# Float32 pair transposes, eight-step tap tiles, merged spectral products and a new order in a one-core convolution and MLP kernel

## The chip, the cores and the metric

The kernel runs on one core of a Trainium2 chip. The metric is the device time of one execution in microseconds. Three runs of the kernel before gave 232.59, 232.85 and 233.19, a median of 232.85.

The engines that matter are TensorE (PE in the profile; its weight loads are PEld), VectorE (DVE), ScalarE (ACT), GpSimd (POOL) and the DMA queue that SyncE (SP) issues. TensorE writes only to the accumulators in PSUM; DVE and ACT bring the results from there into SBUF, which is called evicting.

## The reference

The inputs have 2,048 time steps and 640 channels. The first layer is a convolution block, the second an MLP; both add to their input.

```python
x = A_q
h = x + _A_ref(_layernorm(x, axis=-1), A_k, A_v, A_shift_k, A_ssm_k, A_ssm_D)
h2 = h + _B_ref(_layernorm(h, axis=-1), B_w1, B_b1, B_w2)
# _A_ref: k_shift = sum over 4 taps of k, delayed by 0..3 steps, times shift_k
#         kv = k_shift * v
#         y = causal convolution of kv with ssm_k over the whole length (by FFT) + kv * ssm_D
#         return q * y                  # q is the normalized x
# _B_ref: h = x @ w1 + b1 (1,728 wide); act = h * tanh(softplus(h)); act @ w2
```

## The kernel before, in words

The work is written as named operations (`OP`, `DMA`), each with an engine or a choice of engines, the operations it needs and the buffers it takes. `ORDER` (line 26) is one list of all of them, each with its engine: t is TensorE, a ScalarE, v VectorE, p GpSimd, d the DMA queue of SyncE. `_schedule` (line 141) walks that list with planned durations and gives every operation a planned start; the instructions are then emitted in the order of these starts. So on each engine and on the DMA queue they run strictly in that order, whatever is ready. The planned durations decide only the order.

A time step t is 16*t1 + t2. The 640 channels are five blocks of 128, and three chunks: chunk 0 is block 0, chunk 1 blocks 1 and 2, chunk 2 blocks 3 and 4. The FFT is done as matmuls:

- `k1pe`/`k1ev` (lines 537, 543): each block of the filter is transposed, 16 transposes of 128x128 in bf16, and evicted to `kk_s`. `dadd` adds the D term to it.
- `ktpe`/`ktev`/`ktsh` (493 to 506): k is transposed for the tap convolution, 16 transposes a block, evicted in one operation, and GpSimd copies a shifted edge.
- `wsh` (418): GpSimd builds the tap matrices out of `coef`, which four VectorE casts bring from the matmul `cfpe`.
- `kspe` (512): the tap convolution, per block and half of the time 16 matmuls, eight of 128 columns and eight of 96. `kv` (524) multiplies its PSUM result by v on VectorE and writes `kv_all`.
- `s1k`, `s1v` (456): the first step of the transform of filter and of kv, 20 groups each, evicted as 1,024 columns (`s1kev`, `s1vev`).
- `s2k` (569) and `s2v` (605): the second step with the table `G`, 22 and 20 groups, evicted to `uk` (the filter's spectrum K) and `uv` (the spectrum V).
- `sw` (584): DMAs that swap neighbouring partitions of K into `SW` buffers, which lie in `xa`, `rn` and `rb`.
- `p2`, `p1` (621): VectorE or GpSimd multiplies SW by V in place and then V by K in place, 20 pairs.
- `i1` (656): the inverse transform's first step, 20 groups of 16 matmuls with V and SW as weights, evicted to `Z`, which lies in `uk`. The group of a chunk needs all products of that chunk.
- `i2` (720): the second step, per tile of 128 time steps; `y` evicts it, `wb` multiplies by the normalized x (`lnx`), `h` adds x, `bn`/`pow`/`hc` are the second LayerNorm, `trpe`/`trev` transpose it.
- `ln1`, `ln1p` (695, 702): statistics of the first LayerNorm, per tile two statistics operations, an aggregate and an addition of epsilon on VectorE, and a power and a scaling on GpSimd.
- `m1`/`hb` (786, 802) and `m2`/`res`/`d_out` (812 to 829): the MLP in units of 256, 256, 512, 512 and 512 steps, Mish on ScalarE with its result in `uv`, the residual on VectorE, and the output's DMA. The last tile goes in two halves of 320 columns (832 to 836).

PSUM is four tiles of two banks (`R_PS`): a matmul group takes one, and it comes free when its eviction has ended. `d_id` (379) is the loading of small constants over ScalarE's own queue; `warm` (383) is a Mish activation on two elements, which brings ScalarE's function table.

Of the kernel before, what the change touches and what calls it, by code (L numbers as in the profile page):

```python
# [11 lines left out]
ALU = mybir.AluOpType  # L12
# [4 lines left out]
S = 2048  # L17
D = 640
# [6 lines left out]
EPS = 1e-5  # L25
ORDER = """
cz:v d_id:a wz:v wm:t cfpe:t coef:v d_off:d d_n0:d k1pe0:t d_n2:d k1pe2:t k1ev0:v dadd0:v s1kpe0_0:t k1ev2:v s1kev0_0:a dadd2:v s1kpe0_1:t s1kev0_1:a
s1kpe0_2:t s1kev0_2:v d_n3:d k1pe3:t k1ev3:a dadd3:p d_n1:d k1pe1:t s1kpe2_2:t d_k0:d k1ev1:v s1kpe2_0:t d_k1:d s1kev2_2:a d_n4:d d_k3:d s1kpe2_1:t
s1kev2_1:a d_k2:d s1kpe0_3:t s1kev2_0:v s1kpe3_3:t s1kev3_3:a s1kpe2_3:t d_x0:d s1kev0_3:v s1kev2_3:a dadd1:v s1kpe3_2:t d_g0:d s1kpe3_0:t s1kev3_0:a
s1kpe1_2:t s1kev3_2:v s1kpe1_0:t s1kpe1_1:t k1pe4:t s1kev1_1:a s1kev1_2:v k1ev4:a dadd4:p ktpe1_0:t ktpe1_1:t s1kev1_0:v d_g1:d d_g3:d ktpe1_2:t  # L30
ktpe1_3:t ktev1:v s1kpe1_3:t s1kev1_3:a s1kpe3_1:t s1kev3_1:a d_g4:d w2z:p s1kpe4_0:t s1kpe4_2:t s1kev4_2:a ln1_0:v s1kev4_0:v s1kpe4_1:t s1kev4_1:a
s1kpe4_3:t s1kev4_3:a ktpe0_0:t d_g2:d ktpe0_1:t d_g7:d ktpe0_2:t ktpe0_3:t ktpe3_0:t ktpe3_1:t ktpe3_2:t wsh2:p d_v1:d ln1_3:v ktpe3_3:t wsh1:p
ln1_2:v ktev3:v ktev0:a ktpe4_0:t s2kpe_2:t s2kev_2:a ktpe4_1:t ktpe4_2:t ktsh0:p ktpe4_3:t ktev4:v ktsh3:p s2kpe_9:t ktsh1:p s2kev_9:a d_g5:d
s2kpe_10:t s2kev_10:v s2kpe_0:t s2kev_0:a s2kpe_1:t s2kev_1:a s2kpe_12:t kz:p s2kev_12:v d_v0:d s2kpe_6:t d_a12:d s2kev_6:a ktsh4:p s2kpe_5:t
s2kpe_3:t s2kev_3:a s2kev_5:v ktpe2_0:t ktpe2_1:t d_g6:d ktpe2_2:t ktpe2_3:t ktev2:v s2kpe_21:t wsh0:p s2kpe_8:t s2kev_21:a s2kpe_7:t ln1p0:p ln1p3:p
kspe1_1:t wsh3:p s2kev_8:a s2kpe_4:t s2kpe_19:t s2kev_7:v s2kev_4:a s2kev_19:a kspe2_1:t kv1_1:v s2kpe_11:t kv2_1:v s2kev_11:a sw0_0:d s2kpe_15:t
ktsh2:p s2kev_15:a kspe4_1:t kv4_1:v s2kpe_14:t s2kev_14:a sw1_0:d kspe2_0:t s2kpe_13:t s2kev_13:a s2kpe_16:t kspe1_0:t kv2_0:v s1vpe2_0:t s2kev_16:a
s1vev2_0:a kv1_0:v s1vpe2_2:t s1vev2_2:v s1vpe2_3:t s1vev2_3:a s1vpe1_0:t s1vev1_0:v s1vpe1_3:t s1vev1_3:a s1vpe1_2:t s1vev1_2:a s1vpe1_1:t s1vpe2_1:t
s1vev2_1:a s2kpe_20:t s1vev1_1:v s2kpe_17:t s2kev_17:a s2kev_20:v kspe3_0:t s2kpe_18:t s2vpe1_2:t kspe0_1:t s2kev_18:a s2vev1_2:a sw1_1:d p2_1_2:p
s2vpe1_1:t s2vev1_1:a kv3_0:v s2vpe1_3:t s2vev1_3:a kspe4_0:t ln1_1:v s2vpe1_4:t s2vev1_4:a kv0_1:v kv4_0:v p2_1_3:v s2vpe1_6:t s2vev1_6:a kspe0_0:t  # L40
s2vpe1_0:t s2vev1_0:a p1_1_2:v p1_1_3:p kv0_0:v kspe3_1:t d_x2:d warm:a kv3_1:v sw0_1:d s2vpe1_7:t s2vev1_7:a s1vpe4_1:t s1vev4_1:a p2_1_1:v p2_1_0:v
p1_1_1:v p1_1_0:p s1vpe3_2:t s1vev3_2:a s1vpe0_2:t s1vev0_2:a s1vpe4_0:t s1vev4_0:v s1vpe0_0:t s1vev0_0:a s1vpe3_0:t sw2_0:d s1vev3_0:v p2_1_7:v
s1vpe0_3:t s1vev0_3:a s1vpe0_1:t s1vev0_1:a s1vpe3_1:t s1vev3_1:v s1vpe4_2:t s1vev4_2:a s1vpe3_3:t s1vpe4_3:t s1vev4_3:a s1vev3_3:v s2vpe0_3:t
s2vev0_3:a p1_1_7:p p2_1_6:v sw2_1:d s2vpe2_4:t s2vev2_4:a s2vpe1_5:t s2vev1_5:a s2vpe0_1:t s2vev0_1:a p1_1_6:v p2_1_4:v s2vpe0_0:t p2_0_3:v
s2vev0_0:a p1_1_4:v p1_0_3:v p2_1_5:v p1_1_5:v s2vpe2_0:t p2_0_1:v p1_0_1:v s2vpe2_6:t s2vev2_6:a s2vpe2_5:t s2vev2_5:a s2vev2_0:v s2vpe0_2:t
s2vpe2_3:t s2vev0_2:a i1pe1_4:t s2vev2_3:a i1ev1_4:a s2vpe2_1:t p2_2_0:v p2_0_0:v s2vpe2_7:t s2vev2_7:a s2vpe2_2:t d_w14:d d_w10:d i1pe1_1:t
s2vev2_1:a i1ev1_1:a s2vev2_2:a i1pe1_7:t d_w12:d p1_0_0:v p2_0_2:v p1_0_2:v i1pe0_0:t i1ev0_0:a i1pe0_1:t i1ev0_1:a i1pe0_3:t p2_2_6:v i1ev0_3:a
p2_2_3:v p1_2_3:v p2_2_5:v p1_2_5:v p2_2_1:v p1_2_0:v p1_2_1:v p1_2_6:v i1pe0_2:t d_x1:d i1pe1_5:t p2_2_7:v p1_2_7:v d_w11:d i1ev0_2:a i1pe1_0:t
p2_2_4:v d_w13:d p1_2_4:v i1ev1_7:a i1ev1_5:a i1pe1_3:t i1ev1_3:a d_t2m:d i1ev1_0:a i1pe1_2:t p2_2_2:v p1_2_2:v i1pe1_6:t d_w2:d i1ev1_2:v i1pe2_5:t
i1pe2_7:t ln1_6:v d_small:p i1ev1_6:a gate:p lnx3:a i1ev2_5:a ln1p2:p ln1p1:p ln1_7:v i1ev2_7:a i1pe2_1:t i1ev2_1:a i1pe2_4:t i1ev2_4:v ln1_4:v  # L50
i1pe2_2:t i1ev2_2:a i1pe2_0:t i1ev2_0:a lnx1:p i1pe2_3:t i1ev2_3:v lnx2:p ln1p7:p ln1p6:p lnx6:p i1pe2_6:t ln1_12:v i2pa0:t i2pb0:t i2pa1:t ln1p4:p
i2pb1:t i1ev2_6:a lnx0:p i2pc1:t y1:a i2pc0:t y0:v lnx4:p b1pe:t wb1:v i2pa12:t i2pb12:t c_b1:a i2pc12:t y12:a wb0:v h0:v bn0:v i2pa3:t i2pb3:t
i2pc3:t y3:a i2pa2:t i2pb2:t i2pc2:t h1:p bn1:v i2pa6:t pow0:p hc0:v i2pb6:t y2:a i2pc6:t y6:a i2pa8:t i2pb8:t i2pc8:t y8:a i2pa11:t i2pb11:t i2pc11:t
y11:a i2pa5:t i2pb5:t i2pc5:t y5:a i2pa4:t i2pb4:t i2pc4:t y4:a i2pa13:t i2pb13:t i2pc13:t y13:a i2pa15:t i2pb15:t i2pc15:t y15:a pow1:p trpe0:t hc1:v
wb2:v i2pa7:t trev0:a i2pb7:t trpe1:t i2pc7:t trev1:v y7:a wb3:v i2pa10:t i2pb10:t i2pc10:t y10:a m1pe0_0:t m1pe0_2:t hb0_0:a m1pe0_4:t hb0_4:a
hb0_2:a h2:v bn2:v h3:p bn3:v pow2:p hc2:v m1pe0_1:t hb0_1:a pow3:p hc3:v m1pe0_6:t wb4:v h4:p trpe2:t trpe3:t lnx7:a trev2:v m1pe0_3:t hb0_6:a
ln1_10:v bn4:v ln1_5:v m1pe0_5:t wb7:p h7:p trev3:a m1pe1_1:t m1pe1_3:t wb6:v hb0_3:a h6:v hb1_1:a hb0_5:a ln1p5:p bn6:v m1pe1_4:t lnx5:a pow4:p bn7:v
hb1_3:a wb5:v h5:v bn5:v hb1_4:a m1pe1_6:t hb1_6:a pow7:p pow6:p hc4:v hc6:v hc7:v m2pe0:t trpe4:t trev4:a trpe6:t ln1_8:v trev6:a ln1p8:p ln1p10:p
ln1_11:v m1pe1_0:t ln1p11:p trpe7:t trev7:a res0:v pow5:p hb1_0:a hc5:v lnx10:a wb10:v h10:v m2pe1:t trpe5:t trev5:v m1pe1_5:t lnx11:a m1pe2_2:t
lnx8:a wb8:p h8:p wb11:v h11:v bn11:v res1:v m1pe2_0:t bn8:v pow8:p hc8:v hb2_2:a ln1_15:v ln1p15:p hb1_5:a ln1p12:p lnx12:p bn10:v pow10:p wb12:p  # L60
lnx15:p m1pe2_6:t h12:v bn12:v hb2_6:a m1pe2_5:t hb2_5:a m1pe1_2:t hb2_0:a hb1_2:a m1pe2_3:t hb2_3:a pow12:p ln1_13:v ln1p13:p i2pa9:t pow11:p i2pb9:t
i2pc9:t y9:a m1pe2_1:t hb2_1:a m1pe2_4:t hb2_4:a ln1_9:v ln1p9:p hc11:v lnx13:a lnx9:a wb9:v h9:p trpe8:t trev8:v bn9:v pow9:p m2pe2:t res2:v d_out2:d
trpe11:t d_out0:d hc9:v m2pe3:t res3:v m2pe7:t hc10:v trev11:a res7:v d_out7:d trpe10:t trev10:a trpe9:t trev9:v hc12:v ln1_14:v ln1p14:p lnx14:p
d_out1:d m2pe4:t res4:v d_out4:d wb15:v h15:p bn15:v i2pa14:t i2pb14:t i2pc14:t y14:a d_out3:d wb14:v h14:p m2pe6:t m1pe3_0:t bn14:v pow14:p m1pe3_2:t
res6:v d_out6:d wb13:v h13:v hb3_0:a hb3_2:a bn13:v m1pe3_1:t hb3_1:a trpe12:t m1pe3_5:t hc14:v hb3_5:a pow13:p pow15:p trev12:v m1pe3_6:t hb3_6:a
hc13:v hc15:v trpe15:t trev15:v m1pe3_3:t hb3_3:a trpe14:t trev14:v trpe13:t trev13:a m2pe5:t res5:v d_out5:d m1pe3_4:t hb3_4:a m1pe4_5:t hb4_5:a
m1pe4_4:t hb4_4:a m1pe4_1:t hb4_1:a m1pe4_2:t hb4_2:a m1pe4_3:t hb4_3:a m2pe8:t res8:v d_out8:d m1pe4_6:t hb4_6:a m1pe4_0:t hb4_0:a m2pe10:t m2pe14:t
res14:v d_out14:d res10:v d_out10:d m2pe12:t res12:v m2pe11:t res11:v m2pe13:t res13:v d_out13:d d_out12:d m2pe9:t res9:v d_out9:d d_out11:d m2ape15:t
resa15:v d_outa15:d m2bpe15:t resb15:v d_outb15:d
# [60 lines left out]


_SWITCH = 0.14
_COUNT = [('s1.pe|kspe|k1pe|i1pe', 32), ('ktpe', 8), ('s2kpe_21', 4), ('s2kpe', 12), ('s2vpe0', 64), ('s2vpe1', 32), ('s2vpe2', 32), ('i2pa', 4), ('i2pb', 4), ('i2pc', 8), ('wm', 20), ('trpe', 10), ('m1pe._6', 30), ('m1pe', 20), ('m2pe', 56), ('m2.pe', 28), ('cfpe|b1pe', 2)]
_MARK, _BLOCK, _FETCH, _SLOW = 204, 253, 2.2, 5.0
_PORT_DVE = r"(p[12]_|wsh|dadd|wb|h\d|hc)"
_PORT_POOL = r"(wsh|lnx|ktsh|dadd|p[12]_|wb|h\d|hc|ln1p|pow)"
# [69 lines left out]
def _make_tables():  # L206
# [13 lines left out]
    for dl in range(4):  # L220
        G[0, :, dl, :, 0, :, dl] = c
        G[1, :, dl, :, 0, :, dl] = -s
        G[0, :, dl, :, 1, :, dl] = -s
        G[1, :, dl, :, 1, :, dl] = -c
    T["g"] = np.moveaxis(G, 4, 6).reshape(128, 128 * 128)

    th = 2 * np.pi * g[:, None] * t2[None, :] / 16
    cg, sg = np.cos(th), np.sin(th)
# [648 lines left out]
```

## Time and profile before

| | us |
|---|---|
| median of three runs | 232.85 |
| profiled execution, its own time | 232.84 |
| its span in the profile | 231.1 |
| last spectral product ends (VectorE) | 84.26 |
| last i1 eviction ends (ScalarE) | 92.83 |
| first m1 matmul starts | 101.79 |
| last residuals start | 227.58 |

| engine | busy us | share of the span |
|---|---|---|
| PE | 219.0 | 95% |
| DVE | 145.0 | 63% |
| ACT | 137.8 | 60% |
| POOL | 69.6 | 30% |

A row of a group gives the line, the engine, the operation, what it writes and reads, and behind the bar the busy time, the mean duration in ns and the idle time before it. A duration runs from start to acknowledged end; a second operation right behind it begins a little before that end, so a row's mean is longer than the pace. The granted TensorE clock is 1.00 in every stretch. The 1.74 us between the span and the execution's own time lie outside the profile.

### The profile page before, as it was taken

To read this page: it belongs to the slowest core of one execution; us is meant where nothing else is said; L and a number is where in the kernel's file an instruction comes from. 1 tells how busy PE (TensorE), PEld (TensorE's weight loads), DVE (VectorE), ACT (ScalarE), POOL (GpSimd) and SP (SyncE) were. 2 spreads that over 40 slices of the span, in tenths; PEclk is the share of its full clock that TensorE was granted. 3 is DMA by queue.
4 is the path that set the end of the run, shared out by engine and by line. 5 is a ranking of instruction groups with operands and counts; after the bars stand their busy time and mean duration, and the time that the engine had idled before them with its cause. 6 is when DMAs were issued, how large, how long until landed. Compare 5 with 4: busy or idle time off the path is not lost.

```text
span 231.1 us, 6508 instructions
## 1 busy us (share of the span) xinstructions
PE 219.0 (95%) x2835; PEld 167.3 (72%) x2835; DVE 145.0 (63%) x277; ACT 137.8 (60%) x187; POOL 69.6 (30%) x98
## 2 busy tenths in 40 slices
PE   7999999997889989989999999999999999999993
PEld 2898999897789979878876455777446546577772
DVE  0888999899999998987997837554641100104121
ACT  2399999999999997887745586111355254300000
POOL 0002993036620039446547186305320000000000
PEclk9999999999999999999999999999999999999999
DMA  6999997437966299200000000012000000001012
GB/s 216 380 353 375 427 413 238 129 109 244 291 175 223 54 414 373 84 1 3 0 0 3 1 0 3 24 53 96 19 11 3 28 0 0 31 0 57 3 58 85
DMA packets 19215, 28.74 MB, mean 124 GB/s; under 512 B 1137, under 2 KB 15602, under 8 KB 18802
## 3 DMA queue, kind: packets, MB, share of 16 engines
q1 hardware_dynamic: 18896, 28.17, 34.7%
q8 instruction: 22, 0.36, 0.6%
q10 hardware_dynamic: 194, 0.15, 0.2%
q14 instruction: 7, 0.06, 0.1%
q0 software_dynamic: 96, 0.00, 0.0%
HBM read 20.45 MB, written 2.62 MB: 100 GB/s over the span
## 4 chain that ended last, share of the span: by engine, by line
PE 71%; DVE 18%; ACT 5%; issue 4%; POOL 0%; DVEq 0%
PE ps L818 26%; PE ps L797 25%; ACT uv L372 4%; DVE uv L374 3%; DVE uv L625 3%; DVE uk L374 3%; PE ps L496 2%; DVE rb L629 2%; PE ps L573 2%; PE ps L540 2%; PE ps L762 2%; PE ps L394 2%; PE ps L660 2%; PE ps L661 2%; PE ps L466 2%
## 5 line engine op out<-in xcount | busy, mean ns | idle before, releaser
L818 PE MATMUL ps<-rn,uv 128*128 128x320 bf16 x448 | 62.3, 299 | 0.0
L797 PE MATMUL ps<-G 128*128 128x512 bf16 (+1 forms) x325 | 58.3, 336 | 0.0
L806 ACT ACTIVATE uv<-ps,b1s 128x512 bf16<-128x512 f32 (+1 forms) x70 | 36.7, 592 | 35.7 <-PE ps L797 28.1
L818 PEld LDWEIGHTS <-uv 128*128 128x128 bf16 x448 | 43.5, 98 | 16.9
L372 ACT CAST uk<-ps 128x1024 bf16<-128x1024 f32 (+2 forms) x47 | 43.9, 1061 | 9.0 <-PE ps L467 6.4
L797 PEld LDWEIGHTS <-G 128*128 128x128 bf16 x325 | 31.4, 98 | 23.0 <-issue 0.4
L372 ACT CAST uv<-ps 128x1024 bf16<-128x1024 f32 x32 | 30.2, 1072 | 0.3 <-PE ps L467 0.3
L824 DVE TENSOR_TENSOR xa<-ps,xa 128x640 bf16<-128x640 f32 x6 | 4.9, 823 | 26.7 <-PE ps L818 26.7
L660 PE MATMUL ps<-a,uv 128*128 128x128 bf16 x160 | 18.7, 219 | 1.2 <-DVE uv L625 1.1
L660 PEld LDWEIGHTS <-uv 128*128 128x128 bf16 x160 | 17.9, 113 | 1.3 <-DVE uv L625 1.3
L824 DVE TENSOR_TENSOR xb<-ps,xb 128x640 bf16<-128x640 f32 (+1 forms) x7 | 4.9, 727 | 21.9 <-PE ps L818 21.9
L374 DVE CAST uk<-ps 128x1024 bf16<-128x1024 f32 (+1 forms) x15 | 17.6, 1197 | 1.0 <-PE ps L661 0.6
L749 POOL TENSOR_TENSOR r<-ve,mhalf 128x1 f32<-128x1 f32 x16 | 9.3, 585 | 15.1 <-DVE ve L746 15.1
L703 POOL TENSOR_TENSOR r<-ve,mhalf 128x1 f32<-128x1 f32 x16 | 9.0, 562 | 14.4 <-DVE ve L699 14.4
L609 PE MATMUL ps<-uv,G 128*128 128x64 bf16 (+1 forms) x384 | 12.4, 186 | 1.0 <-issue 0.7
L466 PE MATMUL ps<-cst,ra 128*64 128x128 bf16 x160 | 10.7, 219 | 2.4 <-ACT uv L372 1.3
L525 DVE TENSOR_TENSOR ra<-ps,rb 128x1024 bf16<-128x1024 f32 x10 | 12.0, 1222 | 1.3 <-PE ps L520 1.3
L609 PEld LDWEIGHTS <-G 128*128 128x128 bf16 x384 | 11.6, 96 | 1.3 <-issue 1.1
L372 ACT COPY G<-ps 128x640 bf16<-128x640 bf16 x8 | 5.5, 698 | 11.6 <-PE ps L762 11.6
L372 ACT CAST rb<-ps 128x640 bf16<-128x640 f32 x15 | 9.4, 726 | 4.9 <-PE ps L724 4.9
L625 DVE TENSOR_TENSOR uv<-uv,uk 128x1024 bf16<-128x1024 bf16 x17 | 11.5, 690 | 0.8
L573 PE MATMUL ps<-uk,G 128*128 128x160 bf16 x128 | 10.8, 230 | 0.2
(111 smaller groups left out, 384.2 us busy)
## 6 DMA issues: line engine op xcount, KB each, us to landing
G<-tab_g SPq DMA_DIRECT2D x8, 512.0 KB, 8.2
rn<-in_A_ssm_k_dram SPq DMA_DIRECT2D x5, 512.0 KB, 6.7
ra<-in_A_k_dram SPq DMA_DIRECT2D x4, 640.0 KB, 9.2
rb<-in_A_v_dram SPq DMA_DIRECT2D x2, 1280.0 KB, 14.4
G<-in_B_w_dram SPq DMA_DIRECT2D x5, 432.0 KB, 4.6
rn<-in_B_w_dram SPq DMA_DIRECT2D x1, 2080.0 KB, 12.3
rn<-uk SPq DMA_DIRECT2D x4, 512.0 KB, 4.0
rb<-uk SPq DMA_DIRECT2D x4, 512.0 KB, 8.0
```

The lines of the kernel that those rows point to most:

```text
L372: nc.scalar.copy(o, i)
L374: nc.vector.tensor_copy(o, i)
L466: nc.tensor.matmul(ps[0:64, dgl, :], lhs, mc, start=True, stop=True)
L525: nc.vector.tensor_tensor(kv_w[:, m, :, 8 * h:8 * h + 8, :], rt.tile.rearrange("p (l t d) -> p d t l", l=4, t=8), raw_v[:, 8 * h:8 * h + 8 ...
L573: nc.tensor.matmul(ps[:, o:o + 160], g_v[:, f, :], KA[:, :, f, :], start=True, stop=True)
L609: nc.tensor.matmul(ps[:, fl * st:fl * st + n], g_v[:, f0 + fl, :], V[c.i][:, :, f0 + fl, :], start=True, stop=True)
L625: eng.tensor_tensor(v, v, K[c.i][:, :, f0:f1, :], ALU.mult)
L660: nc.tensor.matmul(pz[:, dgl, :], V[c.i][:, dg // 4, :, dg % 4], a12[:, 0, :], start=True, stop=False)
L797: nc.tensor.matmul(ph[:, i * 512:i * 512 + w], w1[:, dc, fc * P:fc * P + P], lnhT_of(u)[:, dc, 0:w], start=(dc == 0), stop=(dc == NDC - 1))
L806: nc.scalar.activation(hb_of(u)[:, fc, 0:n], rt.tile[:, i * 512:i * 512 + n], ACT.Mish, bias=b1s[:, fc:fc + 1], scale=1.0)
L818: nc.tensor.matmul(po[:, a * 512:a * 512 + 320], hb_of(u)[:, fc, o - x * w // 2:o - x * w // 2 + P], w2[:, fc + x, a * 320:a * 320 + 320], ...
L824: nc.vector.tensor_tensor(x, rt.tile[:].rearrange("p (a d) -> p a d", a=2)[:, n, 0:320], x, ALU.add)
```

## The change

- The filter and k are transposed as float32 words that hold two bf16 neighbours: eight transposes for a block, with a float32 identity `eye`, where there were 16. The filter's pairs are two neighbouring steps; those of k are two neighbouring channels. The columns of `kk_s` and of kv become channel-major with the 16 steps innermost, and the rows of `G` follow.
- The tap tiles are 8 steps by 16 channels. `wsh` becomes five operations of 2x704 elements, one for each block, and lies beside `kt_s` in `uv`. `kspe` has matmuls of 128 and 48 columns, written to every second PSUM column. The shifted copy is two columns further left in the same buffer, so `ktsh` is gone. `coef` comes from six matmuls.
- `uk`, `xa`, `rn`, `rb` and `G` become parts of one tile `mega`. K and SW of a chunk so have one distance, and one operation multiplies both by V, read twice. The products stand in K and SW; V is left free. `i1` reads K and SW, `Z` lies in `uv`, and Mish's result in `uk`.
- `warm` comes first on ScalarE; the constants' queue has two more loads (`eye`, `rep`).
- `ln1` is without the addition of epsilon, which is done with the powers for batches of 2, 2, 4, 4 and 4 tiles.
- On tiles 0 and 1 `wf` reads i2's PSUM result and multiplies it by `lnx` in one operation.
- The last tile goes in pieces of 320, 224 and 96 columns. The load of x's last part no longer needs kspe.
- The order of everything is new. VectorE's list is, up to the last product: cz wz coef k1ev3 k1ev2 dadd1 s1kev0_0 s1kev3_1 s1kev2_0 s1kev0_2 k1ev4 s1kev3_2 ln1_3 ln1_0 s1kev1_2 ktev2 ln1_2 ktev1 ktev0 ln1_1 ktev4 ktev3 kv0_1 kv1_1 kv2_0 kv4_0 kv2_1 kv1_0 kv3_0 kv0_0 kv3_1 s1vev1_0 s2kev_3 s1vev2_0 s1vev1_1 kv4_1 p2_1_4 p2_1_6 s1vev0_3 s1vev3_1 s1vev3_3 s1vev0_1 p2_1_7 s2vev1_1 p2_1_2 s2vev1_3 p2_1_1 p2_1_3 p2_1_0 p2_2_5 p2_0_2 p2_0_3 p2_0_0 p2_0_1 and the other seven of chunk 2. ScalarE begins with d_id warm k1ev0 k1ev1 and then s1kev. TensorE has k1pe0, 3, 1 and 2 ahead of the first s1kpe. The DMA queue: n0 n3 n1 n2 g7 k3 g5 n4 k0 k2 x0 k1 a12 g6 g4 g3 v1 v0 g2 g1 g0, the six sw, x2.

```diff
+    sizes = [P * 160, 4096, NT * D + 1024, NT * D, P * P]
+    mega = big.tile([P, offs[5]], BF16, name="mega")
+    uk, xa, rn, rb, gt = [mega[:, offs[i]:offs[i + 1]] for i in range(5)]
...
-        Z.append(k.rearrange("p (j d) -> p j d", d=c.w))
+        KP.append(mega[:, a:a + 2 * d].rearrange("p (z o) -> p z o", z=2)[:, :, 0:P * c.ng].rearrange("p z (b f g) -> p z b f g", f=P, g=4))
+        Z.append(uv[c.i].rearrange("p (j d) -> p j d", d=c.w))
...
-                for gl in range(4):
-                    nc.tensor.transpose(ps[:, gl, a, :], raw_k[:, a * 4 * D + b * 4 + gl:(a + 1) * 4 * D:20], ident)
+                for l in range(2):
+                    c = 4 * h * D + 10 * r + 2 * b + l
+                    nc.tensor.transpose(ps[:, l, r, h, :], raw_k.bitcast(F32)[:, c:(h + 1) * 4 * D:20], eye[:])
...
-                    for a in (2 * h, 2 * h + 1):
-                        o = ps[:, l * 256 + (a - 2 * h) * P:][:, 0:P]
-                        nc.tensor.matmul(o, t[:, l, a, :], wsh[r // 5][:, r % 5, 0:128], start=True, stop=False)
-                        nc.tensor.matmul(o[:, 0:96], t[:, l, a - 1 if a else 4, :], wsh[r // 5][:, r % 5, 128:224], start=False, stop=True)
+                    for r in range(2):
+                        nc.tensor.matmul(ps[:, l * 256 + r:l * 256 + 256:2], t[:, l // 2, r, h, 8:136, l % 2], wsh[m][:, r, l, 0:128], start=True, stop=False)
+                        nc.tensor.matmul(ps[:, l * 256 + r:l * 256 + 96:2], t[:, l // 2, r, 1 - h, 8 - (1 - h):136 - (1 - h), l % 2], wsh[m][:, r, l, 128:176], start=False, stop=True)
...
-                nc.vector.tensor_tensor(kv_w[:, m, :, 8 * h:8 * h + 8, :], rt.tile.rearrange("p (l t d) -> p d t l", l=4, t=8),
-                                        raw_v[:, 8 * h:8 * h + 8, :, 4 * m:4 * m + 4].rearrange("p t d l -> p d t l"), ALU.mult)
+                nc.vector.tensor_tensor(kv_w[:, m, :, :, 8 * h:8 * h + 8], rt.tile.rearrange("p (l t d) -> p d l t", l=4, t=8),
+                                        raw_v[:, 8 * h:8 * h + 8, :, 4 * m:4 * m + 4].rearrange("p t d l -> p d l t"), ALU.mult)
...
-            for t2 in range(NT):
-                nc.tensor.transpose(ps[:, t2, :], n[:, t2:S:16], ident)
+            for t2 in range(8):
+                nc.tensor.transpose(ps[:, t2, :], n.bitcast(F32)[:, t2:S // 2:8], eye[:])
...
-                    eng.tensor_tensor(v, v, K[c.i][:, :, f0:f1, :], ALU.mult)
-                    return
-                for b, t in SW[c.i]:
-                    k = t[:, :, f0:f1, :]
-                    eng.tensor_tensor(k, k, v[:, b:b + t.shape[1]], ALU.mult)
+                kp = KP[c.i][:, :, :, f0:f1, :].rearrange("p z b f g -> p z b (f g)")
+                v = V[c.i][:, :, f0:f1, :].rearrange("p b f g -> p b (f g)").unsqueeze(1).to_broadcast([P, 2, c.ng // 4, 4 * (f1 - f0)])
+                (nc.gpsimd if e == "pool" else nc.vector).tensor_tensor(kp, kp, v, ALU.mult)
...
+            if fused:
+                nc.vector.tensor_tensor(v(tt_rt.tile), rt.tile[:, 0:D].rearrange("p (b d l) -> p b d l", b=5, l=4), v(lnx_rt.tile), ALU.mult)
+                return
```

## Prediction before the run

> **What bounds the kernel now.** I read the page's totals and slices first, then the busy times in chosen stretches, then the chain that ended last in order of time, then the groups with their shapes kept apart, and last the VectorE and ScalarE timelines for the pace of one operation behind another.
>
> ```profile
> span 231.1 us, 6508 instructions
> PE 219.0 (95%) x2835; PEld 167.3 (72%) x2835; DVE 145.0 (63%) x277; ACT 137.8 (60%) x187; POOL 69.6 (30%) x98
> ```
>
> ```profile
> 30.00:40.00 10.00, 9.85 (x161) 9.52 (x160) 9.00 (x9) 9.20 (x12) 6.49 (x8) 1.00 0.87 319
> 40.00:50.00 10.00, 9.58 (x250) 8.98 (x248) 9.01 (x12) 9.42 (x11) 0.41 (x1) 1.00 0.33 92
> ...
> 70.00:80.00 10.00, 9.86 (x195) 9.49 (x192) 9.69 (x15) 10.00 (x13) 0.00 (x0) 1.00 0.46 144
> ...
> 105.00:228.00 123.00, 122.54 (x882) 79.19 (x879) 53.37 (x134) 47.12 (x84) 30.31 (x43) 1.00 0.06 21
> ```
>
> The columns are the length, then busy PE, PEld, DVE, ACT and POOL, the granted clock, the DMA share and GB/s. The average (PE 95%, DVE 63%) misleads. From 105 us on TensorE has work without a gap, and nothing in the change takes work from that half; it can only be shifted. Up to 92 us, where the convolution is done, PE, DVE and ACT all stand at 90 to 100%, so a microsecond added to one list is not absorbed by the others, and most of the change is there.
>
> ```profile
> 83.57 0.70 DVE uv L625
> 84.32 0.25 PE ps L660
> ...
> 91.73 0.07 PE ps L661
> 91.82 1.02 ACT uk L372
> ```
>
> In the chain, the last spectral product ends on VectorE at 84.26 us; only then can the eight i1pe2 groups go (to 91.62), and i2, LayerNorm and the MLP follow. So the date of the last product dates the rest.
>
> ```profile
> L525 DVE TENSOR_TENSOR ra<-ps,rb 128x1024 bf16<-128x1024 f32 x10 | 12.0, 1222 | 1.3 <-PE ps L520 1.3
> L374 DVE CAST uk<-ps 128x1024 bf16<-128x1024 f32 x10 | 11.9, 1220 | 0.9 <-PE ps L661 0.6 <-PE ps L467 0.2
> L625 DVE TENSOR_TENSOR uv<-uv,uk 128x1024 bf16<-128x1024 bf16 x17 | 11.5, 690 | 0.8
> L540 PEld LDWEIGHTS <-rn 128*128 128x128 bf16 x80 | 5.5, 149 | 0.3
> L519 PEld LDWEIGHTS <-uv 128*128 128x128 bf16 x80 | 7.7, 97 | 0.1
> L660 PEld LDWEIGHTS <-uv 128*128 128x128 bf16 x160 | 17.9, 113 | 1.3 <-DVE uv L625 1.3
> ```
>
> ```profile
> 78.25 1.89 DVE L625 TENSOR_TENSOR uv<-uv,uk 128x1024 bf16<-128x1024 bf16 x3
> 49.55 2.35 DVE L525 TENSOR_TENSOR ra<-ps,rb 128x1024 bf16<-128x1024 f32 x2
> 59.07 12.96 ACT L372 CAST uv<-ps 128x1024 bf16<-128x1024 f32 x14
> 54.06 1.28 ACT L385 ACT_TABLE_LOAD   x1
> ```
>
> The paces: a product half (1.89-0.69)/2 = 0.60; kv or a 1024-column eviction on DVE 1.13; on ACT (12.96-1.07)/13 = 0.92.
>
> **The change, part by part.**
>
> *kv (L525).* Now it walks time innermost, so each element of v is read 640 elements (1,280 bytes) after the last; before, four neighbours were read together. No row has VectorE reading SBUF so. Lower end: nothing, because single-element hops in its PSUM operand already cost nothing (1222 against the 1220 of the plain cast); a gain is excluded, the count of elements is the same. Upper end: weight loads from SBUF, 97 ns dense, 113 at 8 bytes' step, 149 at 32 bytes: a factor of 1.52, or 0.52x1.22 = +0.63 a kv. I take the upper end, as the nearest row that reads SBUF: 1.76 a kv, +6.3 for ten. The Trainium skill's Vector Engine (DVE) Microarchitecture Reference (5.2 Measured stream behaviour on trn2) has 1.73 ns a column with one source hopping every element, 1.054 without; by that, as an estimate, 10x1024x0.68 ns = +6.9 instead of +6.3. No trace here shows it yet.
>
> *Products.* 17 DVE halves of V*K and 19 of V*SW, with 4 on POOL, become 20 merged ones, 19 on DVE and one on POOL. The half runs two elements a ns nearly; 1024 elements more at (0.69-0.48)/384 us (the 0.48 is L735's 640-element row at 100.45) add 0.55, so one takes 1.15 for 2x0.60. But POOL now takes one product, not four halves, so DVE's go from 36x0.60 = 21.6 to 19x1.15 = 21.9. POOL's one of some 4.8 (two of 2.38) must end before i1 of chunk 1 and has 10 us.
>
> *Eviction lists.* DVE to ACT: s2kev 5 to 1 on DVE, s1kev 7 to 6; ACT to DVE: one ktev, one s2vev. DVE loses about 3.5, ACT's net is +0.9 and it is relieved of the table load and warm activation at 54 us (-1.5), which move to its idle start (ACT idles till 9.69).
>
> *LayerNorm 1.* DVE loses the 0.15 ve operation of each tile; POOL has 5 batches for 16. A batch waits for its last tile; the first units use batches 0 to 2, ready as their tiles are.
>
> *TensorE.* k1 and kt: 160 bf16 transposes at 71 ns (16 in 1.14 at 18.39) become 80 in float32. Lower end 71 each (-5.7), upper end 205 if the strided load of 149 no longer hides behind the 56 of the stream (+5.0). I take 120: -1.8. kspe: a pair of 128+96 columns takes 98 ns; now 128+48 into every second PSUM column. Lower end 83 (-1.2 for ten), upper end each 128 costing as much as 256 columns do (112 ns, 30 in 3.44 at 101.79): 154 a pair, +4.5. I take the middle, +1.5, for nothing in the trace writes PSUM in steps. The Trainium skill's PSUM — Partial Sum Buffer (Specifications (TRN2)) says that any non-contiguous pattern slows matmuls significantly; by that the +4.5 would stand. No run here shows it.
>
> *Start.* Two more loads on ACT's queue (0.36 to 0.59 each) put sk_r about 0.85 later, at some 1.95 with 3.8 to land = 5.75; PE is in its warm-up until 5.85, so cfpe and the k1pe0 behind it lose 0 to 1. Five more matmuls and 0.4 of coef lie in DVE's idle time before 8 us. All four k1pe now stand before the first s1kpe, which so starts near 10.8, not 9.0; ACT has two k1ev done by then.
>
> *POOL and queues.* Five wsh of 2.07x1408/1120 = 2.6 against four, without five ktsh of 0.61: +1.7 on an engine at 30%; wsh1 is ready near 30 us, its first reader runs near 34. If it were late, kspe and all of PE's queue would wait. SP: x0 still waits for s1kpe2, now with k1 and then a12, g6, g4, g3, v1, v0 behind it; v lands near 30 us (11.1 MB at 0.4 MB/us and 2 of latency), kspe needs it near 34. x2 no longer waits for kspe, but stands behind sw0.
>
> *Fused tiles, tail.* wf takes one 0.83 DVE read for an eviction and a product (0.7+0.48) on two tiles, beside 14 tiles of i2 on PE: nothing. At the end the two last residuals ran together after the last matmul (0.89 at 227.58); 224 and 96 columns at 1.05 ns a column make about 0.55: -0.3. The pieces' matmuls cost 0.04 more.
>
> *Sum along VectorE.* (a) s1k ends on ACT: 11.3 + 14x0.92 + 0.8 = 25.0 (before 26.6). (b) Five ktev 5.7, two ln1 2.1, nine kv 15.8: 48.6. (c) Ten evictions 11.3, one kv 1.8, seven products 8.1, to the last of chunk 1: 69.8. (d) Twelve products 13.8: 83.6. Before, DVE idled about 3.6 from 27 to 84; I keep 3.0: 86.6, against 84.26: +2.3. TensorE in (b): 40 transposes 4.8, 21 s2kpe 8.8 (12 matmuls in 0.83), nine kspe 8.3: 46.9, under DVE. The i1 groups, 20x0.9 from 71.8, end under 86.6+7.3 = 93.9. So 232.84 + 2.3 - 0.3 = 234.8. The profiled execution's own 232.84 is the median's 232.85.
>
> **Rivals.** *One: v's hops cost nothing.* For it, PSUM's hops are free. Then (b) takes 17.9 and DVE is through at 80.9; ACT bounds: 11.3 + 75.1 (14 s1kev, 13 s1vev, 18 s2vev, 18 i1ev at 0.92 or a little more, 20 s2kev at (6.79-1.00)/7 = 0.83 from the eight at 27.61, one of 0.4) + its idle of before, 3.4, = 89.8 for the last i1 eviction, before 92.84: -3.0 - 0.3, 229.5. It decides at about 0.4 more a kv: below that the kernel is faster. Against it, the weight loads' 113 and 149.
>
> *Two: TensorE becomes the bound of (b).* Transposes at 205 and kspe at 1.23: 8.2+8.8+11.1 from 25.0 = 53.1, 4.5 behind DVE's 48.6: 239.3; with kspe alone at 1.23 and transposes at 120, 49.7, 1.1 more, 235.9. For it, the chain already runs through L519 and L573 from 31 to 41 us. Against it, one transpose carries what two did.
>
> *Three: the merged product loses its double pace, because V is read twice with a step of 0.* Then 2048 elements take about 2.3 (1.22 + 1024 at 1.05 ns), +1.1 on 19: some 255. The step of 0 is not the innermost, which is as dense as before, so it is unlikely.
>
> **How the numbers follow.** Forecast 0.48 (own range 231.8 to 236.8: idle 1 to 5, cfpe's 0 to 1); rival one 0.28 (its idle spreads it to 228.5 to 231.5); rival two 0.20; rival three 0.04. The predicted time is 234.8. The range 229.2 to 239.0 leaves a tenth or less on either side. A measurement of this kernel tells 0.3%, 0.7, from no change. Faster: 0.25 of rival one, 0.09 of the forecast's low end: 0.34. Same: 0.10 (forecast 0.07, rival one 0.03). Slower: 0.56.
>
> **What would show it.** kv near 1.85 us each, not 1.22; DVE's last product near 86.6; ACT with idle before s1vev. Rival one: kv at 1222, the last i1 eviction near 89.8. Rival two: kspe's first matmuls 112 apart, transposes over 150, DVE waiting for L520's successor. It would be wrong if the new order left other gaps than those kept, in the second half above all, or if the one large tile made waits that the separate ones didn't.

## The result and the profile after

| | median of runs, us | lowest to highest | profiled execution | its span | mean granted clock |
|---|---|---|---|---|---|
| before | 232.77 | 232.59 to 233.19 | 232.84 | 231.1 | 1.000 |
| after | 290.17 | 289.84 to 291.11 | 291.11 | 289.2 | 0.911 |

The changed kernel takes 1.247 times as long (95% interval 1.2435 to 1.2503): 57 us more, where 2 more were forecast. In two of the later runs one execution (245.83 and 238.50 us) fell in a slower state with a granted clock of 0.986, and their medians and ranges leave it out. The page of the profile after, its totals and two of its slice rows:

```profile
span 289.2 us, 6326 instructions
...
PE 240.6 (83%) x2768; PEld 188.8 (65%) x2774; DVE 148.8 (51%) x241; ACT 139.9 (48%) x187; POOL 63.7 (22%) x80
...
PE   5798997489325766565799999999999999999995
...
PEclk9799999689875979656599999999999999999999
```

VectorE has 148.8 us of work, 3.8 more than before, and ScalarE 2.1 more. Neither makes 57. TensorE's row has its holes between 43 and 145 us; the second half is as dense as it was, but its first m1 matmul runs at 159.95, not 101.79. The stretches (length, then busy PE, PEld, DVE, ACT, POOL, granted clock, DMA share, GB/s) show no engine full:

```profile
40.00:50.00 10.00, 8.41 (x109) 7.93 (x107) 6.23 (x4) 6.52 (x7) 0.00 (x0) 1.00 0.23 64
50.00:60.00 10.00, 5.29 (x38) 5.29 (x38) 5.57 (x3) 1.92 (x2) 0.00 (x0) 0.66 0.16 44
...
80.00:90.00 10.00, 1.27 (x29) 1.07 (x28) 7.63 (x4) 1.42 (x2) 6.81 (x4) 0.67 0.57 156
...
120.00:130.00 10.00, 6.29 (x56) 5.50 (x55) 3.68 (x3) 4.13 (x5) 0.00 (x0) 0.50 0.01 2
130.00:140.00 10.00, 5.19 (x52) 4.39 (x49) 3.51 (x3) 4.05 (x4) 0.00 (x0) 0.67 0.73 283
```

So these are waits. VectorE's, from 40 to 145 us (total, times, longest):

```profile
DVE mega L642 <- PE ps L672: 12.3, 7, 2.3
DVE ra L543 <- DMA mega<-mega: 11.4, 2, 6.5
DVE mega L642 <- DMA mega<-mega: 10.2, 2, 5.6
DVE mega L642 <- DMA mega<-in_A_q_dram: 5.0, 1, 5.0
```

L543 is kv, L642 the merged product, "mega<-mega" a swap transfer, L671 and L672 the i1 matmuls. kv multiplies PSUM by v, which lies in rb; a swap transfer of chunk 1 reads uk and writes rn. They share no element, yet one waits for the other. The last row is a load of x for a later stage, for which a product waits. The chain shows both kinds. First, a swap transfer waits for a kv, and the next kv for that transfer; later, products and i1 take turns:

```profile
44.38 1.95 DVE ra L543
46.45 0.65 SPq L606
47.15 5.50 DMA mega<-mega
52.77 1.90 DVE ra L543
...
120.88 1.24 DVE mega L642
122.17 0.29 PE ps L672
...
124.06 1.24 DVE mega L642
...
127.17 1.24 DVE mega L642
```

A product starts every 3.1 us there, though it takes 1.24. Part of that is the lower clock: the i1 matmuls between two products take 1.8 us at a granted clock of 0.50, where a group took 0.9 in the kernel before. A product of chunk 2 writes K of chunk 2 in uk and its copy in rb, as one operand with a step from one to the other. Between the two lie xa and rn, which the i1 groups of chunks 0 and 1 read. The groups of operations whose prices the prediction had to bound:

```profile
L642 DVE TENSOR_TENSOR mega<-mega,uv 128x2048 bf16<-128x2048 bf16 x19 | 26.6, 1424 | 28.6 <-PE ps L672 12.3
L543 DVE TENSOR_TENSOR ra<-ps,mega 128x1024 bf16<-128x1024 f32 x10 | 19.0, 1923 | 15.3 <-DMA mega<-mega 11.4
```

kv takes 1923 ns, where 1.85 was to be seen; five products behind one another took 5.76 at 103.80, so (5.76-1.22)/4 = 1.135 each, where 1.15 was.

### The profile page after: what moved, and what is told of

It is laid out like the page before. It is cut to its first block, busy times and chain, and to the rows that moved or that the text cites. A ratio compares the mean times of both kernels' runs of the same rounds, so it can differ in the third digit from the quotient of the medians.

```text
span 289.2 us, 6326 instructions
## 1 busy us (share of the span) xinstructions
PE 240.6 (83%) x2768; PEld 188.8 (65%) x2774; DVE 148.8 (51%) x241; ACT 139.9 (48%) x187; POOL 63.7 (22%) x80
## 4 chain that ended last, share of the span: by engine, by line
PE 64%; DVE 12%; DMA 11%; issue 4%; ACT 4%; POOL 2%; SPq 1%; ACTq 0%; DVEq 0%; POOLq 0%
PE ps L847 21%; PE ps L821 19%; DMA mega<-mega 7%; DVE mega L642 6%; PE ps L672 4%; DVE ra L543 3%; PE ps L671 3%; PE ps L742 3%; ACT uv L386 3%; PE ps L591 2%; PE ps L520 2%; DMA sk_r<-in_A_shift_k_dram 2%; DMA mega<-in_A_q_dram 2%; PE ps L537 2%; PE ps L786 2%
## 5 line engine op out<-in xcount | busy, mean ns | idle before, releaser
L386 ACT CAST uv<-ps 128x1024 bf16<-128x1024 f32 x49 | 47.0, 1028 | 42.0 <-PE ps L672 17.1
L847 PE MATMUL ps<-mega 128*128 128x320 bf16 (+2 forms) x462 | 62.4, 295 | 0.0
L821 PE MATMUL ps<-mega 128*128 128x512 bf16 (+1 forms) x319 | 57.5, 336 | 0.3
L847 PEld LDWEIGHTS <-mega 128*128 128x128 bf16 x462 | 44.2, 98 | 16.1 <-issue 0.2
L830 ACT ACTIVATE mega<-ps,b1s 128x512 bf16<-128x512 f32 (+1 forms) x70 | 36.6, 592 | 26.9 <-PE ps L821 24.1
L386 ACT CAST mega<-ps 128x960 bf16<-128x960 f32 (+3 forms) x46 | 39.0, 912 | 16.4 <-PE ps L591 15.0
L821 PEld LDWEIGHTS <-mega 128*128 128x128 bf16 x325 | 31.3, 98 | 23.8 <-issue 0.4
L642 DVE TENSOR_TENSOR mega<-mega,uv 128x2048 bf16<-128x2048 bf16 x19 | 26.6, 1424 | 28.6 <-PE ps L672 12.3
L672 PE MATMUL ps<-a,mega 128*128 128x128 bf16 x160 | 26.3, 261 | 9.5 <-DVE mega L642 9.5
L671 PE MATMUL ps<-a,mega 128*128 128x128 bf16 x160 | 26.7, 262 | 3.8 <-DVE mega L642 3.3
L672 PEld LDWEIGHTS <-mega 128*128 128x128 bf16 x160 | 20.2, 128 | 11.4 <-DVE mega L642 11.2
L543 DVE TENSOR_TENSOR ra<-ps,mega 128x1024 bf16<-128x1024 f32 x10 | 19.0, 1923 | 15.3 <-DMA mega<-mega 11.4
L671 PEld LDWEIGHTS <-mega 128*128 128x128 bf16 x160 | 20.4, 128 | 4.2 <-DVE mega L642 3.5
L627 PE MATMUL ps<-uv,mega 128*128 128x64 bf16 (+1 forms) x384 | 14.5, 199 | 9.1 <-DVE ra L543 4.5
L627 PEld LDWEIGHTS <-mega 128*128 128x128 bf16 x384 | 13.6, 105 | 9.7 <-issue 9.5
L591 PEld LDWEIGHTS <-mega 128*128 128x128 bf16 x128 | 10.7, 106 | 6.9 <-issue 6.8
```

The source lines that it names most:

```text
L386: nc.scalar.copy(o, i)
L543: nc.vector.tensor_tensor(kv_w[:, m, :, :, 8 * h:8 * h + 8], rt.tile.rearrange("p (l t d) -> p d l t", l=4, t=8), raw_v[:, 8 * h:8 * h + 8 ...
L591: nc.tensor.matmul(ps[:, o:o + 160], g_v[:, f, :], KA[:, :, f, :], start=True, stop=True)
L627: nc.tensor.matmul(ps[:, fl * st:fl * st + n], g_v[:, f0 + fl, :], V[c.i][:, :, f0 + fl, :], start=True, stop=True)
L642: (nc.gpsimd if e == "pool" else nc.vector).tensor_tensor(kp, kp, v, ALU.mult)
L671: nc.tensor.matmul(pz[:, dgl, :], K[c.i][:, dg // 4, :, dg % 4], a12[:, 0, :], start=True, stop=False)
```

## Experiments

**Theory A**: the 57 us are waits between operations that touch no common element, made by putting uk, xa, rn, rb and gt into one tile, and most of them by the merged product's reach. **Rival B**: the new order and the new operations are slow themselves. **Rival C**: the lower clock is a cause. The diffs are shortened: `...` stands for what is left out, and calls are abridged. In a timeline's row the bracket gives the idle time before, and what ended it.

### Five tiles and split products

```diff
-    mega = big.tile([P, offs[5]], BF16, name="mega")
-    uk, xa, rn, rb, gt = [mega[:, offs[i]:offs[i + 1]] for i in range(5)]
+    uk, xa, rn, rb, gt = [big.tile([P, n], BF16, name=x)[:] for x, n in ...]
...
-                tensor_tensor(kp, kp, v, ALU.mult)
+                for x in (SW[c.i][0][1], K[c.i]):
+                    kp = x[:, :, f0:f1, :]
+                    tensor_tensor(kp, kp, v, ALU.mult)
```

> The changed kernel with uk, xa, rn, rb and gt as five tiles again, and each product as two operations (V*SW, then V*K) at the same place of the same order; all else as changed. Theory A: the loss is waits between operations that touch no common element, made by the one large tile. They go, the granted clock is back at 1.0, and what is left is the sum of the prediction with kv at the measured 1.92 (+1.6 for ten), transposes at 0.165 and kspe pairs at 0.153 (TensorE then 1 to 2 behind VectorE's list): 236 to 241 us. Rival B: the new order and the new operations cost the time themselves: 270 us or more, with waits in the same places. Rival C: a slower TensorE clock is a cause and not a consequence: the clock stays near 0.91 with the same matmuls, 280 or more.

Measured 243.09 us (241.95 to 244.01), 1.0445 times the kernel before (1.0407 to 1.0484): 47 of the 57 us are gone with the order unchanged, and the clock is back at 0.986. B and C fall as the main cause, though C adds its part where products and i1 take turns. It is 2 above the range expected. VectorE's timeline:

```profile
38.26 17.54 DVE L539 TENSOR_TENSOR ra<-ps,rb 128x1024 bf16<-128x1024 f32 x9 [0.88 <-PE ps L534]
```

VectorE's row of nine kv now has no gap. What is left is 10.4 us, taken apart below.

### The tile kept, the products split

Only the second half of the diff above.

> The changed kernel with the one large tile kept, and only the merged products undone (two operations each, each inside its own part of the tile). Theory A1: most of the loss is that one operation that reaches from K to SW spans what lies between them; then the alternation of i1 and products from 109 to 140 us goes, and only kv's two waits for the swap transfers (6.3 and 7.2 us in the chain of the changed kernel) are left: 245 to 255 us. Theory A2: any use of one tile is enough: 285 or more.

One run: 255.62 us, against 290.17 and 243.09. Its waits on VectorE:

```profile
DVE ra L543 <- DMA mega<-mega: 12.1, 2, 7.1
```

No product waits for i1 or for a transfer in its list. By this single run, the merged product's reach costs 290.2-255.6 = 34.6 us, and the one tile by itself 255.6-243.1 = 12.5, which is kv's two waits for swap transfers (12.1).

### The kernel before, on one tile

```diff
+    mega = big.tile([P, offs[5]], BF16, name="mega")
+    uk, xa, rn, rb, gt = [mega[:, offs[i]:offs[i + 1]] for i in range(5)]
```

> The kernel before with its five tiles uk, xa, rn, rb and gt made views of one tile, nothing else. Theory A: kv reads v in rb, and the swap transfers write rn and xa in every second partition; now three kv wait for them and they for kv: 238 to 252 us. Rival: one tile costs nothing by itself, 232.8.

250.16 us (249.81 to 250.52), 1.0755 times before (1.0727 to 1.0784). Not one operation differs from the kernel before, only who waits (VectorE's waits, and those of the DMA queue). That it is the swap transfers' writes to every second partition which join them to kv was not tried, and stays open.

```profile
DVE ra L524 <- DMA mega<-mega: 15.7, 3, 6.0
```

```profile
SPq L587 <- DVE ra L524: 20.2, 2, 15.5
```

### Where the last 10 us are: the start

```diff
-        nc.scalar.dma_start(eye[:], ...)
-        nc.scalar.dma_start(cst[:], ...)
-        nc.scalar.dma_start(rep[:], ...)
         nc.scalar.dma_start(sk_r[:], ...)
+        nc.scalar.dma_start(rep[:], ...)
+        nc.scalar.dma_start(eye[:], ...)
+        nc.scalar.dma_start(cst[:], ...)
```

> The changed kernel with five tiles and split products (243.1), and only the order of four loads on ScalarE's queue changed: shift_k, rep, eye, cst instead of eye, cst, rep, shift_k. Theory: TensorE idles from 6.16 to 8.07 until shift_k lands, and the granted clock of 0.5 from 9.5 to 13.2 us follows from that idle time; without it the 32 float32 transposes take less than their 5.46, s1k starts near 10.5 instead of 13.8, and the time falls by 2 to 3.3: 239.8 to 241. Rival: the low clock has another cause (the float32 transposes themselves); then it is still 0.5 somewhere before 15 us and the gain is 0 to 1.9.

This run and the next four stand on five tiles with split products. TensorE's timeline with five tiles, and then with shift_k first as well:

```profile
8.38 5.46 PE L554 MATMUL ps<-eye,rn 128*128 128x128 f32 x32
```

```profile
6.83 3.97 PE L554 MATMUL ps<-eye,rn 128*128 128x128 f32 x32 [1.01 <-DMA eye<-tab_eye]
```

And the stretch from 10 to 14 us of each:

```profile
10.00:14.00 4.00, 4.00 (x29) 3.88 (x29) 1.39 (x3) 2.71 (x2) 1.49 (x2) 0.61 1.02 409
```

```profile
10.00:14.00 4.00, 3.41 (x90) 3.01 (x90) 3.14 (x4) 3.71 (x4) 3.09 (x4) 1.00 1.03 414
```

In these two executions the theory fits: shift_k lands 1.6 us after its issue when it is first, 6.2 in the changed kernel, where it stands fourth. TensorE idles 1.0 us (now for `eye`) instead of 1.9, the granted clock is 1.00, not 0.61, and 32 transposes take 3.97. s1k starts at 11.29 instead of 13.76. That the idle time is the cause is not shown, for two runs below speak against it as the whole account. The run with all three edits, and then the one with v read densely (its transposes and its stretch from 10 to 14 us):

```profile
7.08 5.43 PE L554 MATMUL ps<-eye,rn 128*128 128x128 f32 x32 [0.45 <-DMA eye<-tab_eye]
```

```profile
10.00:14.00 4.00, 3.66 (x62) 3.47 (x62) 2.68 (x3) 3.26 (x3) 1.67 (x3) 1.00 1.02 414
```

```profile
8.87 6.42 PE L554 MATMUL ps<-eye,rn 128*128 128x128 f32 x32
```

```profile
10.00:14.00 4.00, 4.00 (x20) 4.00 (x20) 1.74 (x3) 1.87 (x1) 0.85 (x2) 1.00 1.01 397
```

The first has only 0.45 us of idle time and is slow, and both are slow while the record of the granted clock says 1.00. Over the profiled executions with float32 transposes, the 32 took 5.1 to 6.4 us in all five with 1.9 to 2.7 us of idle time, and about 4 in three of the four with shift_k first. So the idle time goes with the slow start, but something else can make it too, and what does stays open.

For the time the theory does not hold: 242.21 us (241.99 to 243.30) against 243.09, with ranges that overlap. The first kv starts only 1.5 earlier (36.74 for 38.26), and TensorE waits twice in between (1.2 in all) for POOL's addition of D to the filter (L563).

### v read densely

```diff
-  kv_w[...] , rt.tile "p (l t d) -> p d l t", raw_v "p t d l -> p d l t"
+  kv_w[...] "p d l t -> p d t l", rt.tile "p (l t d) -> p d t l", raw_v "p t d l -> p d t l"
```

> Five tiles, split products, and kv walked with the four neighbours of v innermost (v read densely as before the change, the result written in steps of 16 elements). Theory: the 0.7 that a kv takes more than before is v's hop of 640 elements; kv falls from 1.94 to about 1.22, VectorE's list before the last product by up to 7, but TensorE's kspe then bound that part: 236 to 240.5. Rival: the hop of the result costs as much as that of v, kv stays at 1.9, 243.

268.98 us, 26 more. Both theory and rival missed: the step has gone from the source to the result, and there it costs far more.

```profile
L539 DVE TENSOR_TENSOR ra<-ps,rb 128x1024 bf16<-128x1024 f32 x10 | 43.6, 4654 | 1.9 <-PE ps L534 1.9
```

### kspe's PSUM columns dense

```diff
-  ps[:, l * 256 + r:l * 256 + 256:2]
+  ps[:, r * 512 + l * 128:r * 512 + l * 128 + 128]
```

The matmuls of 48 columns change in the same way, and kv reads the columns where they now lie.

> Five tiles, split products, and kspe's matmuls write 128 and 48 neighbouring PSUM columns (the two parities in two banks, kv reads them so) instead of every second one. Theory: the step in PSUM makes the pair 153 ns; dense it is 98 or less, TensorE loses 4.4 in ten kspe, of which VectorE's list, whose nine kv run without a gap, passes on little: 240.5 to 243. Rival: the pair is slow because its weights are read in steps of two elements (134 ns a load against 97 before); the pair stays near 153, 243.

240.98 us (240.43 to 242.5), 2.1 less; the ranges overlap a little, the intervals do not (1.0317 to 1.0372 times the kernel before, against 1.0407 to 1.0484). The chain's matmuls of 128 columns, first with the step (five tiles), then dense:

```profile
36.95 0.11 PE ps L533
37.10 0.11 PE ps L533
37.26 0.11 PE ps L533
```

```profile
37.93 0.06 PE ps L533
38.01 0.06 PE ps L533
38.09 0.06 PE ps L533
```

```profile
L533 PEld LDWEIGHTS <-uv 128*128 128x128 bf16 x80 | 6.8, 97 | 0.1
```

A pair comes every 0.15 us with the step and every 0.08 without. The weights (last fence, with dense columns) are still read in steps of two elements, and take 97 ns: the rival is out, the step in PSUM was the cause. The edit also spreads the pairs over two banks, but 0.08 is what the 98 ns of the kernel before make for 176 columns instead of 224, so nothing is left for that. TensorE now waits for kv, which with the step it did only once (0.5 us):

```profile
38.67 16.75 DVE L539 TENSOR_TENSOR ra<-ps,rb 128x1024 bf16<-128x1024 f32 x9 [0.31 <-PE ps L534]
```

```profile
PE ps L587 <- DVE ra L539: 2.9, 7, 0.6
```

kv now comes every (16.75-1.94)/8 = 1.85 us. With the step it came every (17.54-1.94)/8 = 1.95, and TensorE, busy for 17.20 of the 18 us from 38 to 56, set that pace; with dense columns it is busy for 14.11 of them.

### All three edits

> All three edits together (loads in the order shift_k, rep, eye, cst; v read densely; kspe's PSUM columns dense), on five tiles with split products. If each theory holds, TensorE and VectorE both lose what they lost: 3 at the start, and 5 to 7 in the part with kspe and kv: 232 to 236, level with the kernel before. If the hop of kv's result costs what v's did, or kspe's weights are the cause, 238 to 241.

266.0 us (265.39 to 266.78): again the result's step (kv 4645 ns). Neither expected range held.

### The hop taken away

kv with other data, dense in source and result; loads and kspe as in the two edits that helped.

```diff
-  raw_v[:, 8 * h:8 * h + 8, :, 4 * m:4 * m + 4].rearrange("p t (d r) l -> p d r l t", r=2)
+  rb[:, (2 * m + h) * 1024:(2 * m + h) * 1024 + 1024].rearrange("p (d r l t) -> p d r l t", r=2, l=4, t=8)
```

> Five tiles, split products, loads in the order shift_k, rep, eye, cst, kspe's PSUM columns dense, and kv multiplies by 1,024 neighbouring elements of v instead of its own (the product is thus another one; all else is computed). Theory: what is then left of the loss is v's hop: kv falls from 1.94 to 1.22, VectorE's last product from about 93 to 86, and the time to 233 to 236. Rival: another part of the new order binds as well (ScalarE's evictions or TensorE in the part with kspe); kv falls, but the time stays at 237 or more.

233.47 us (232.47 to 235.91), 1.007 times before (1.0035 to 1.0104), and kv is back at its old price:

```profile
L539 DVE TENSOR_TENSOR ra<-ps,rb 128x1024 bf16<-128x1024 f32 x10 | 11.9, 1221 | 1.8 <-PE ps L534 1.8
```

No run has the same two edits alone with v's own data. The nearest is the next one, which also merges chunk 2's products: against it the hop is worth 240.1-233.5 = 6.6 us of the time, of the 7.2 that it adds to VectorE's list. By their paces the merged products save some 0.5 (eight times 0.06), so the 6.6 is good to about a microsecond. All the rest of the change, with the start and kspe mended, is then 0.9 us above the kernel before by the medians, 1.6 by the ratio. Even that is not in every execution: the five at a granted clock of 0.999 or 1.000 took 232.47 to 233.47, level with the kernel before, the four at 0.993 234.49 to 235.91.

### Merging neighbours

```diff
-    uk, rb = two tiles
+    ukrb = big.tile([P, sizes[0] + sizes[3]], BF16, name="ukrb")
+    uk, rb = ukrb[:, 0:sizes[0]], ukrb[:, sizes[0]:sizes[0] + sizes[3]]
...
+                if c.i == 2:
+                    kp = ukrb[:, 12288:28672] "p (z b f g) -> p z b f g" [:, :, :, f0:f1, :]
+                    tensor_tensor(kp, kp, v twice, ALU.mult)
```

> Five tiles but uk and rb as one, loads in the order shift_k, rep, eye, cst, kspe's PSUM columns dense; the products of chunk 2 merged as in the change, those of chunks 0 and 1 split. K of chunk 2 and its swapped copy lie next to each other there, so the merged operation spans nothing else. Theory: not the merging but what lies between makes the waits: products of 1.14 behind one another, no alternation with i1, and the time of the two edits without merging, 238 to 241. Rival: any merged product makes waits: 245 or more.

240.08 us (238.41 to 240.9), as expected. The last five merged products run behind one another at (5.77-1.22)/4 = 1.14:

```profile
85.64 5.77 DVE L641 TENSOR_TENSOR ukrb<-ukrb,uv 128x2048 bf16<-128x2048 bf16 x5 [0.82 <-ACT uv L384]
```

Merging is not what waits; what lies between the parts is.

### Back to the kernel before

```diff
-... d_x2:d warm:a kv3_1:v ...
+cz:v d_id:a warm:a wz:v ...
```

> The kernel before with only the activation that loads ScalarE's table moved from 54 us to the start, where the engine idles. ScalarE is 100% busy from 50 to 60 us, so 1.5 us leave its list: if the list bounds there, 231.3; if VectorE's does, as the chain's last product has it, 232.7. Nothing is expected to become slower.

231.41 us (230.8 to 231.67), 0.9947 times before (0.9929 to 0.9965): 1.2 of the 1.5 taken from ScalarE show in the time, as the expectation had it if ScalarE's list bounds. Then chunk 2's products were merged on neighbouring parts as well:

```diff
-                if which == 0: v *= K
-                SW *= v
+                if c.i == 2: ukrb (K and SW as neighbours) *= v twice, one operation
```

Chunk 2's products then stand in K and SW: i1 reads them there, `Z` of chunk 2 lies in `uv`, and one of Mish's buffers in `uk`.

> The kernel before with that activation at the start, and chunk 2's two products per slice as one operation, on uk and rb as one tile in which they are neighbours (the kernel before otherwise). Eight times 1.20 become eight times 1.14 on VectorE just ahead of the last i1 groups, 0.5 less: 0.3 to 0.6 below the run with the activation alone. Rival: the shared tile brings waits of kv on the swap transfers, 235 or more.

230.38 us (229.16 to 231.01), 0.9893 times before (0.9866 to 0.992), 1.0 below the run with the activation alone, where 0.3 to 0.6 was expected; the two ranges of times overlap a little. Seven products behind one another:

```profile
73.70 8.03 DVE L628 TENSOR_TENSOR ukrb<-ukrb,uv 128x2048 bf16<-128x2048 bf16 x7
```

The last product ends at 81.73, 0.5 earlier than in the profiled execution with the activation alone (82.22), which is what was expected; where the rest of the 1.0 comes from is open. This version takes 1.1% less than the kernel before, and so is faster than both kernels.

## Why the prediction was wrong

The sign was right, and for a part (kv's hop, about 6.6 us) for the reason given; the size was not: 234.8 forecast, at most 239.0, and 290.2 measured. The step that failed is the sum along VectorE, where it keeps 3.0 us of idle time from before. From 27 us to the end of the last product, at 140.2, VectorE was busy for 65.98 of 113.2 us: 47 us idle. The prediction costed the one tile at nothing and named it only in its last sentence, as a wait that might come. It was to be costed where "Products" turns two operations into one: the new operand reaches over three other buffers, and those who use them could have been listed from the diff, with their places in the order. An end for that cost was there too: each of the products of chunks 0 and 2 standing between i1 groups pays a round trip to TensorE and back.

Taken by its steps:

- **kv.** Right in kind, 0.09 too small. The upper end, a pace of 1.76, was taken; it came out at 1.85 where VectorE sets the pace (kspe dense), with a duration of 1.94. Rival one, hops that cost nothing, is out: the hop was worth about 6.6 us of time. The Trainium skill's Vector Engine (DVE) Microarchitecture Reference (5.2 Measured stream behaviour on trn2) has 1.73 ns a column for one source that hops 4 KiB at every element; the trace has 1.9, so it agrees in kind. For a result it gives 1.71 with hops of 4 KiB and 2.50 with steps of 24 words, in elements of 4 bytes. Here a result in steps of 32 bytes, in elements of 2, took 4654/1024 = 4.5 ns, so the measurement decides for this case.
- **Products.** 1.135 for a forecast 1.15; rival three is out. The gain per pair over 1.20 is 0.07, for which the change paid 34.6.
- **TensorE.** kspe: the middle was taken, where the upper end of 154 holds; the lower, 83, is what dense columns take, and 2.1 us of time came back with them. The Trainium skill's PSUM — Partial Sum Buffer (Specifications (TRN2)) says that any non-contiguous pattern slows matmuls significantly; this is what the run with dense columns shows. Transposes: 120 taken, 124 measured in the faster starts (3.97 for 32), but 165 in the part with s2k (1.32 for eight).
- **Start.** Wrong by 2.7: sk_r was put at 5.75, and its reader started at 8.42: it stood behind three loads instead of one on its queue. Then the 32 transposes took 5.46 instead of some 4. s1k was to start near 10.8; it started at 13.76 with five tiles.
- **Eviction lists.** The activation at the start was right: alone, in the kernel before, it is worth 1.2 us.
- **POOL and queues.** The swap transfers were given no cost. Two of them waited for a kv, and the next kv for them (12.5 us).
- **Tail.** -0.3 was forecast. The residuals fell from 0.89 to 0.56, but from the last matmul's end to the end of the span it is 3.5 in both (227.56 to 231.1, 285.64 to 289.2): nothing.
- **Without the waits**, with five tiles, the mechanism forecast as likeliest and rival two came together: VectorE has hardly a gap from the first kv on, 38.26 to 95.3, but TensorE dates that first kv and, with the step in PSUM, sets the pace of the nine. 243.1 is past both, since kv, kspe and the start all came in at or above their upper ends.

## What to carry to other kernels

An operation that joins two buffers through a step also claims what lies between them, wherever waits are made by region: list who reads and writes that stretch, and join only neighbours. Before several buffers become views of one tile, look for transfers and operations that then meet in it without sharing anything. Loads put ahead of a small one that TensorE waits for cost the wait and, in every trace with that wait here, slower matmuls after it; but the time of the whole kernel hardly showed it. Price both ends of an elementwise operation's steps before choosing the walk: here a step in the result added 3.4 us, one in the source 0.7.

## What the runs showed of the hardware that was not expected

- VectorE, one PSUM source in float32 and one bfloat16 source, 1,024 columns: 1.22 us with dense SBUF operands, 1.94 with a source hopping 1,280 bytes at every element, 4.65 with the result written 32 bytes apart.
- Matmuls of 128 and 48 columns into every second PSUM column came every 0.15 us a pair, into neighbouring ones every 0.08.
- 32 float32 transposes at the start took about 4 us in three profiled executions and 5.1 to 6.4 in six: in all five with 1.9 to 2.7 us of idle TensorE before them, and in one with 0.45. In two of the six the recorded granted clock is 1.00 (in the others it sinks, to a mean of 0.61 from 10 to 14 us with five tiles), so a matmul can be slow there while that record shows nothing.
